# Cosine linear attention and a squared-ReLU MLP: batch 0's later queries behind w_in on GpSimd's queue, first products in halves of depth, casts on GpSimd, a new order

## The chip, the cores and the metric

The kernel runs on one core of a Trainium2 chip. The metric is the time in microseconds on the device; several runs give a median, and one further run is recorded by the profiler. Names of engines: PE is TensorE (PEld its weight loads), DVE is VectorE, ACT is ScalarE, POOL is GpSimd, SP is SyncE.

## The reference

```python
batch, n_heads, seq, head_dim = (8, 8, 576, 64)
pos = np.arange(S); theta = np.pi / 2.0 * pos / S
def phi(x, c, s):
    r = np.maximum(x, 0.0)
    return np.concatenate([r * c, r * s], axis=-1)
q_p, k_p = phi(q, cos, sin), phi(k, cos, sin)
kv = np.einsum('bhsf,bhsd->bhfd', k_p, v)
z = np.sum(k_p, axis=2)
num = np.einsum('bhsf,bhfd->bhsd', q_p, kv)
den = np.einsum('bhsf,bhf->bhs', q_p, z)[..., None] + 1e-06
x = (num / den).transpose(0, 2, 1, 3).reshape(B * S, H * D)      # 4608 x 512
h = np.maximum(x @ w_in, 0.0)                                    # w_in 512 x 2048
out = (h * h) @ w_out                                            # w_out 2048 x 512
```

Inputs and output are float32; the products run in bfloat16.

## The kernel before

The eight batches pass one after the other, each through an attention part and an MLP part, and the attention of later batches is interleaved with the MLP of earlier ones. A batch has 576 rows: four main tiles of 128 rows (j = 0 to 3; in the code J is 4) and a tail of 64 (j = 4). k, v and q of a batch are loaded in float32, one main transfer (1 MB, `load_main`, L355) and two tail transfers of 64 KB (`load_tail`, L363) each. There is one buffer for each of k, v and q.

*Attention.* `declare_feature` (L507) makes relu(x) times cos or sin in bfloat16 (tiles kp and qp), on ACT (L406) or DVE (L408). `declare_v` (L520) casts v to bfloat16 (vx), on ACT or DVE (L413); a column of ones beside it gives the sum z. `declare_kz` (L530) forms kv and z on PE, `declare_num` (L605) multiplies the transposed query features with them and divides (den and x, L637 to L639). Queries and x are transposed on PE for batches 0 and 1 (L591, L682) and by DMA on SP's queue later (L575, L667).

*MLP.* `declare_plain` (L712) is a group of the first product: 256 columns of the hidden layer (two blocks hb of 128) for half a batch's main rows (256 rows), eight matmuls of 256 columns, over the four blocks of depth. ACT takes the ReLU (rt, L416), DVE squares it into gT (L419). Batch 0 has 16 groups: hb = 0, 2, ... 14 for its first half of rows, then for its second. The first two groups are split by rows into matmuls of 128 columns, so that each 128 rows of x can start. From batch 3 on a form with seven products in place of eight takes over (`declare_seven1`, L810), with sums of blocks on DVE (w1s, xs; L427). `declare_rows` (L998) is batch 0's second product with w_out (w2sb), in steps of two hidden blocks for each of four row tiles, 64 matmuls of 512 columns; later batches use `declare_pair` (L922), seven products with sums gs and w2s.

*Loads of the start.* `prologue` (L1069) issues on SP: k, k's tail, q's first half (tiles 0 and 1), v's tail, v in two halves of heads, q's second half (tiles 2 and 3), q's tail. GpSimd's queue waits for v's tail by a one-element copy (L1090) and then issues w_in in quarters of 512 hidden columns (L373), which are cast to bfloat16 on the way. Then, on the same queue: batch 1's q and its tail, w_out's first quarter (L380), batch 1's k, w_out's second quarter, batch 1's v, the other quarters of w_out, batch 2's loads, and batch 0's two stores. Batches 3 to 7 load through SP. PE gets filler matmuls (`fill`, L1094) in the start, which write to a spare bank.

*What sets the order.* Operations are not issued as declared: a planner (`Planner`, L52 to L230) has a cost for each operation on each engine it may run on, due times (`pos`, `late`), buffers and a model of the loads, lays all on a time line, and the instructions are written out in that order (L1303 on), so every engine's stream is fixed when the program is built. `SHIFTS` (L21) moves single operations' due times or ties them to one engine. For the first loads the planner is given landing times by hand:

```python
for i in range(4):
    given([("w1", i)], 11.7 + 0.01 * i, size=2.6)
```

In `Planner.plan` a transfer's end follows from those planned before it:

```python
pipe = max(o.end + o.land, pipe) + o.size
o.done = pipe + (self.margin if e != "GIVEN" else 0.0)
```

An engine works through its stream in turn; what waits holds back what is behind it on that engine.

Of the kernel before, what the change touches and what calls it, by code (L numbers as in the profile page):

```python
# [21 lines left out]
23:9.5:ACT 37:-0.5 38:1.0 44:17.5:ACT 46:-1.0 53:-0.5 62:11.5 79:-2.0 85:-2.5 89:3.0 93:11.0  # L22
108:5.5 144:9.0 152:-2.0 157:9.5:ACT 191:-5.0 194:-1.0 202:-1.5 203:-3.5:ACT 204:2.0 210:3.0
238:2.5 241:2.5 243:5.0 249:-6.0 257:-4.0 260:-2.0 261:-6.0 270:2.5 271:3.5 287:-5.0 325:-2.0
335:-0.5 340:1.5 348:8.5 354:-7.0 364:-19.0 383:1.0 390:-3.5 392:1.0 417:-4.5 487:-5.0 492:1.5
516:-7.5 517:-5.5 530:39.0 533:25.5 546:9.0 563:5.5 565:12.5 573:-8.5 575:5.0 588:13.0 593:4.5
598:-2.0 611:-4.5 617:-5.5 636:-1.5 670:7.5 677:-2.0 690:1.0 698:0.0:DVE 702:22.5 703:-19.5
704:3.5:ACT 706:-4.0 715:2.0 731:-2.5 748:5.0 781:-4.5 783:-6.0 785:-7.0 787:-2.0 790:-1.0
794:-1.5 797:1.0 799:1.0 807:11.0 813:-5.5 817:-4.0 820:-7.0 822:-5.5 836:-3.5 850:-3.5
859:-34.0 860:-15.0 870:1.0 872:-4.0 884:12.0 890:49.0 893:17.0 906:5.5 907:23.5 911:3.0 917:3.0  # L30
936:-3.0 951:-12.5 957:-1.0 958:-1.5 963:-3.5 985:7.0 990:-4.0 998:3.5 1005:-4.5 1009:5.5
1023:-10.0 1024:-8.5 1030:-10.0 1041:-26.0:ACT 1042:-10.5 1133:-13.0 1143:1.5 1155:4.0 1157:3.0
1176:-4.5 1191:4.5 1209:5.5 1247:2.5 1306:-0.5
# [200 lines left out]
def kernel(  # L234
# [191 lines left out]
    def sub(out, in0, in1, op=ALU.subtract):  # L426
        nc.vector.tensor_tensor(out=out, in0=in0, in1=in1, op=op)  # L427
# [18 lines left out]
    T1, T2, t = {}, {}, 16.4  # L446
# [11 lines left out]
    def declare_load(b, nm, eng, pos=None, after=()):  # L458
        src = {"k": k, "v": v, "q": q}[nm]
        queue = nc.sync if eng == "SP" else nc.gpsimd  # L460
        for part, fn, cost, size, held in (
            (nm, load_main, 0.65 if eng == "SP" else 0.9, 3.1 if eng == "SP" else 2.7, 5.8),
            (nm + "t", load_tail, 1.3, 0.42, 6.8),
        ):
            buf = loaded[part, b] = plan.buf(part)

            def load(_, fn=fn, buf=buf):
                fn(src, nm, buf.i, b, queue)

            add((eng, cost), load, w=[buf], pos=pos, size=size, after=after, held=held if eng == "SP" else None)  # L470
# [49 lines left out]
    def declare_v(b, j, engs):  # L520
        buf = cached(vxb, (b, j), "vx" if j < J else "vxt")
        n = 1 if j < J else 0.65
        cost = {"ACT": 0.52 * n, "DVE": 0.34 * n}

        def cast(eng):
            copy(eng, at(buf)[:, :, 0:D], piece("v", b, j))
# [815 lines left out]
```

## Time and profile before

| what | value |
|---|---|
| runs | 277.44, 277.49 (median), 277.59 us |
| profiled execution | 276.82 us |
| its span | 274.8 us |
| granted TensorE clock | 1.0 throughout |
| first product with w_in on PE | 16.45 us from the span's start |
| first product with w_out on PE | 33.5 us |
| last product on PE | ends at 271.4 us |
| DMA: one quarter of w_in, issue to landing (median) | 10.5 us |
| DMA: one quarter of w_out, issue to landing (median) | 11.6 us |
| ACT cast of v, 128x512 | 26 at 636 ns |
| DVE cosine feature of q, 128x512 | 29 at 492 ns |
| DVE product of two bfloat16 tiles, 128x1024 | 686 ns |

All times inside the execution count from the span's start. "Busy" is the time in which an engine executes; waiting, and issuing DMAs, is not counted, except that GpSimd's DMA instructions stand among its busy time. In a timeline, a line has the start, the length, the engine, the kernel's line, the operation, what it writes and reads, its shape and how many are merged; in brackets is the idle time of the engine ahead of it, and what ended that. In a table of stretches the columns are: the stretch, its length, busy time of PE, PEld, DVE, ACT and POOL (with instruction counts), the granted clock, the mean share of the DMA engines, GB/s.

### The profile page before, as it was taken

The page shows a single profiled execution, that of the slowest core. Times are in us where ns is not written, and L with a number is a line of the kernel's source. Part 1 is how long each engine was busy: PE and PEld are TensorE (multiplying, and loading weights), DVE is VectorE, ACT ScalarE, POOL GpSimd, SP SyncE. Part 2 cuts the span into 40 slices and gives each one's busy share as a digit, 9 for nine tenths or more (in the row PEclk, how much of TensorE's full clock was granted, in tenths as well). Part 3 has the DMA queues.
Part 4 walks back from the last instruction along what each step waited for, and adds up shares of the span by engine and source line. Part 5 has one row for each costly group of instructions (what it writes and reads, how often), then busy time and mean ns, then how long its engine had stood idle before and what let it go on. Part 6 is the DMA issues. An engine that isn't in the chain of part 4 may idle for free.

```text
span 274.8 us, 7115 instructions
## 1 busy us (share of the span) xinstructions
PE 267.9 (98%) x2845; PEld 227.6 (83%) x2845; DVE 218.9 (80%) x515; ACT 194.9 (71%) x391; POOL 21.6 (8%) x38
## 2 busy tenths in 40 slices
PE   8979999999999999999999999999999999999994
PEld 3668856789988988888888898988988888888884
DVE  1789996997694989699968999799968798279652
ACT  3876982997895598589957994699735954684522
POOL 1453544010000000000000000000000000000000
PEclk9999999999999999999999999999999999999999
DMA  7999999969979998899299955996198301200025
GB/s 217 321 205 290 296 283 365 219 218 225 361 160 186 281 334 156 224 347 221 81 164 308 259 181 102 265 338 217 35 205 170 91 2 44 95 16 2 1 79 153
DMA packets 81840, 53.01 MB, mean 193 GB/s; under 512 B 53584, under 2 KB 77648, under 8 KB 81808
## 3 DMA queue, kind: packets, MB, share of 16 engines
q1 hardware_dynamic: 75136, 40.12, 58.4%
q0 software_dynamic: 6528, 12.32, 17.1%
q8 instruction: 22, 0.36, 0.5%
q10 hardware_dynamic: 144, 0.13, 0.1%
q14 instruction: 10, 0.08, 0.1%
HBM read 36.70 MB, written 9.44 MB: 168 GB/s over the span
## 4 chain that ended last, share of the span: by engine, by line
PE 80%; DMA 8%; DVE 7%; issue 1%; SPq 1%; POOL 1%; ACT 1%; DVEq 0%
PE banks L430 79%; DMA w1sb<-in_moe_w_in_dram 4%; DMA qpT<-qp 2%; DMA vt<-in_v_dram 2%; DVE rs L422 2%; DVE gT L419 2%; DVE gs L427 2%; PE banks L591 1%; DVE x L639 1%; POOL w1sb L373 1%; SPq L366 0%; PE banks L682 0%; DVE qp L408 0%; DVE kp L408 0%; SPq L358 0%
## 5 line engine op out<-in xcount | busy, mean ns | idle before, releaser
L430 PEld LDWEIGHTS <-w1sb 128*128 128x128 bf16 x784 | 73.0, 98 | 10.4 <-DMA w1sb<-in_moe_w_in_dram 1.4
L430 PE MATMUL banks<-xT,w1sb 128*128 128x256 bf16 (+1 forms) x576 | 68.4, 267 | 1.0 <-DMA w1sb<-in_moe_w_in_dram 1.0
L430 PEld LDWEIGHTS <-gs 128*128 128x128 bf16 x512 | 49.0, 98 | 5.9 <-DVE gs L427 0.2
L416 ACT ACTIVATE rt<-banks 128x512 bf16<-128x512 f32 x64 | 37.2, 600 | 14.9 <-PE banks L430 9.3
L430 PEld LDWEIGHTS <-gT 128*128 128x128 bf16 x400 | 38.0, 98 | 9.0
L430 PE MATMUL banks<-w2sb,gT 128*128 128x256 bf16 (+1 forms) x288 | 44.2, 296 | 0.0
L430 PEld LDWEIGHTS <-w1s 128*128 128x128 bf16 x320 | 30.7, 98 | 3.7
L430 PE MATMUL banks<-w2sb,gs 128*128 128x256 bf16 x256 | 33.0, 273 | 0.0
L430 PE MATMUL banks<-w2s,gs 128*128 128x256 bf16 x256 | 32.2, 273 | 0.0
L422 DVE CUSTOM_DVE_ANT_0 rs<-banks,sums 128x512 bf16<-128x512 f32 x40 | 27.0, 684 | 4.5 <-ACT sums L847 3.1
L419 DVE TENSOR_TENSOR gT<-rs 128x1024 bf16<-128x1024 bf16 (+1 forms) x50 | 27.7, 579 | 1.8 <-ACT rs L416 1.0
L416 ACT ACTIVATE rs<-banks 128x512 bf16<-128x512 f32 x40 | 23.6, 604 | 3.1 <-PE banks L430 2.9
L430 PE MATMUL banks<-xs,w1s 128*128 128x256 bf16 x160 | 23.0, 273 | 0.0
L430 PE MATMUL banks<-xT,w1s 128*128 128x256 bf16 x160 | 22.9, 273 | 0.0
L419 DVE TENSOR_TENSOR gT<-rt 128x512 bf16<-128x512 bf16 x48 | 19.2, 418 | 4.5 <-ACT rt L416 4.3
L427 DVE TENSOR_TENSOR ysb<-banks,sums 128x256 f32<-128x256 f32 x32 | 13.4, 418 | 11.2 <-PE banks L430 7.3
L406 ACT ACTIVATE qp<-q,sin_col 128x512 bf16<-128x512 f32 x31 | 22.1, 738 | 0.1
L639 DVE TENSOR_TENSOR x<-banks,den 128x512 bf16<-128x512 f32 x30 | 20.7, 691 | 1.0
L406 ACT ACTIVATE kp<-k,sin_col 128x512 bf16<-128x512 f32 x30 | 21.2, 734 | 0.0
L427 DVE TENSOR_TENSOR gs<-gT 128x1024 bf16<-128x1024 bf16 x28 | 19.2, 686 | 1.1 <-PE banks L430 0.7
L413 ACT CAST vx<-v 128x512 bf16<-128x512 f32 x26 | 16.2, 636 | 0.9 <-DMA v<-in_v_dram 0.9
L637 DVE TENSOR_SCALAR den<-banks 128x8 f32<-128x8 f32 (+1 forms) x38 | 6.0, 159 | 12.5 <-PE banks L430 12.3
(106 smaller groups left out, 364.0 us busy)
## 6 DMA issues: line engine op xcount, KB each, us to landing
out_dram<-ysb SPq DMA_DIRECT2D x13, 512.0 KB, 3.5
k<-in_k_dram SPq DMA_DIRECT2D x6, 1024.0 KB, 6.4
v<-in_v_dram SPq DMA_DIRECT2D x5, 1024.0 KB, 7.9
q<-in_q_dram SPq DMA_DIRECT2D x5, 1024.0 KB, 9.3
w1sb<-in_moe_w_in_dram POOLq DMA_DIRECT2D x4, 512.0 KB, 10.5
q<-in_q_dram POOLq DMA_DIRECT2D x2, 1024.0 KB, 11.2
w2sb<-in_moe_w_out_dram POOLq DMA_DIRECT2D x4, 512.0 KB, 11.6
k<-in_k_dram POOLq DMA_DIRECT2D x2, 1024.0 KB, 11.3
```

The costliest lines, as they stand in the source:

```text
L373: nc.gpsimd.dma_start(out=w1sb[:, :, f0:f1], in_=moe_w_in[:, f0:f1].rearrange("(kb p) f -> p kb f", p=P),)
L406: nc.scalar.activation(out=dst, in_=src, func=ACTF.Relu, scale=col)
L413: (nc.scalar.copy if eng == "ACT" else nc.vector.tensor_copy)(out=out, in_=in_)
L416: nc.scalar.activation(out=out, in_=in_, func=ACTF.Relu)
L419: nc.vector.tensor_tensor(out=out, in0=in_, in1=in_, op=ALU.mult)
L422: nc.vector._custom_dve(TENSOR_ADD_SAT, out=out, in0=in0, in1=in1, s0=float("inf"), s1=0.0)
L427: nc.vector.tensor_tensor(out=out, in0=in0, in1=in1, op=op)
L430: nc.tensor.matmul(out=out, lhsT=lhsT, rhs=rhs, start=start, stop=stop, skip_group_check=True)
L591: nc.tensor.transpose(t[:, h, :], qp_at(b, j)[:, h, :], ident[:, :])
L637: nc.vector.tensor_single_scalar(out=d, in_=n4[:, :, :, D], scalar=EPS, op=ALU.add)
L639: nc.vector.tensor_tensor(out=x_at(b, j).rearrange("p (b k) (l d) -> p b k l d", b=n, l=2), in0=n4[:, :, :, 0:D].rearrange("p b (k l) d -> ...
```

## The change

- *Loads.* SP no longer loads batch 0's q tiles 2 and 3 and the q tail. GpSimd's queue loads w_in in four eighths and two quarters, and q's second half and tail stand behind the first two eighths. The key of a w_in piece (`w1_key`) follows the new pieces.
- *First products.* Batch 0's first two groups are split into three parts each: the first half of depth for all 256 rows, then the second half of depth for each 128 rows.
- *Casts.* `declare_v` may cast on GpSimd (a multiplication by 1.0, twice), and from batch 2 on does nothing else; the cosine features of q may run on ACT as well as on DVE.
- *Stores.* Batch 0's two stores go through SP.
- *Planner.* The costs, sizes and given landing times are other numbers; a load of q on SP follows those of the k and v tails; batch 3's loads are declared k, v, q; `SHIFTS` is another list.

In the built program DVE has 500 instructions instead of 515, ACT 376 instead of 391, and PE 2836 matmuls instead of 2846 (two fillers and eight products fewer). 9 cosine features of k and 9 of q (128x512) move from DVE to ACT. GpSimd has 30 casts, 24 of 128x512 and six tails. On PE's stream the first two products with w_out now stand ahead of the last four groups with w_in; before, all 16 groups stood ahead of the first.

```diff
-    T1, T2, t = {}, {}, 16.4
+    T1, T2, t = {}, {}, 15.2
...
-        cost = {"ACT": 0.52 * n, "DVE": 0.34 * n}
+        cost = {"ACT": 0.52 * n, "DVE": 0.34 * n, "POOL": 0.75 * n}
 
         def cast(eng):
-            copy(eng, at(buf)[:, :, 0:D], piece("v", b, j))
+            if eng == "POOL":
+                nc.gpsimd.tensor_scalar(
+                    out=at(buf)[:, :, 0:D], in0=piece("v", b, j), scalar1=1.0, scalar2=1.0, op0=ALU.mult, op1=ALU.mult
+                )
+            else:
+                copy(eng, at(buf)[:, :, 0:D], piece("v", b, j))
...
+    def w1_key(hb):
+        return ("w1", hb // 2 if hb < 8 else 2 + hb // 4)
...
-        for c in range(2) if split else (None,):
+        whole = (0, KB, 0, TP, 0.0)
+        parts = [whole]
+        if split and b == 0:
+            parts = [(0, KB2, 0, TP, 0.0), (KB2, KB, 0, P, 4 * PROD1), (KB2, KB, P, TP, 4.5 * PROD1)]
+        elif split:
+            parts = [(0, KB, 0, P, 0.0), (0, KB, P, TP, PROD2)]
+        for k0, k1, c0, c1, later in parts:
...
     def st_name(b):
-        return "SP" if b >= 1 else "POOL"
+        return "SP" if b >= 0 else "POOL"
...
-    def declare_att(b, kpos, npos, cos_k=BOTH, cos_q=DVE1, cast=ACT1):
+    def declare_att(b, kpos, npos, cos_k=BOTH, cos_q=BOTH, cast=("POOL",)):
...
-    SPARE, SPARE_UNTIL = 5, 16.0
+    SPARE, SPARE_UNTIL = 5, 14.0
...
-            (k, "k", 0), (k, "kt", 0), (q, "q", 0), (v, "vt", 0), (v, "v", 0), (v, "v", 1), (q, "q", 1), (q, "qt", 0)
+            (k, "k", 0), (k, "kt", 0), (q, "q", 0), (v, "vt", 0), (v, "v", 0), (v, "v", 1)
...
         nc.gpsimd.tensor_copy(out=w1sb[0:1, 0, 0:1], in_=mem["vt"][0:1, 0, 0, 0:1])
-        for i in range(4):
+        for i in range(2):
+            load_w1(i, 8)
+        load_main(q, "q", 0, 0, nc.gpsimd, [slice(J // 2, J)])
+        load_tail(q, "q", 0, 0, nc.gpsimd)
+        for i in range(2, 4):
+            load_w1(i, 8)
+        for i in range(2, 4):
             load_w1(i, 4)
...
-        ([(L("v"), 1)], 12.15), ([(L("q"), 1)], 14.2), ([L("qt")], 14.6),
+        ([(L("v"), 1)], 12.3), ([(L("q"), 1)], 16.7), ([L("qt")], 17.1),
     ):
         given(keys, t, lat=0.0)
-    for i in range(4):
-        given([("w1", i)], 11.7 + 0.01 * i, size=2.6)
+    for i, t in enumerate((13.9, 15.2, 18.4, 19.7, 22.3)):
+        given([("w1", i)], t, lat=0.0)
+    given([("w1", 5)], 20.1, size=2.6)
...
-    declare_att(2, T2[1], [T2[1] + 1.7 + 1.75 * i for i in range(NS)], BOTH, BOTH, BOTH)
-    for nm in "qkv":
+    declare_att(2, T2[1], [T2[1] + 1.7 + 1.75 * i for i in range(NS)], BOTH, BOTH, ("POOL",))
+    for nm in "kvq":
         declare_load(3, nm, "SP", after=[turned["q", 2, J // 2]])
...
-    t0 = {"PE": 8.0, "ACT": 6.3, "DVE": 6.3, "SP": 10.0, "POOL": 12.9, "GIVEN": 0.0}
+    t0 = {"PE": 8.0, "ACT": 6.3, "DVE": 6.3, "SP": 10.0, "POOL": 16.0, "GIVEN": 0.0}
```

## The prediction

> **What bounds the kernel now.** I read the page's first part and a table of stretches first, to see whether TensorE (PE) ever waits; then its waits in order of time; then the DMAs that end them.
>
> ```profile
> PE 267.9 (98%) x2845; PEld 227.6 (83%) x2845; DVE 218.9 (80%) x515; ACT 194.9 (71%) x391; POOL 21.6 (8%) x38
> ```
>
> ```profile
> 16.45:33.50 17.05, 16.03 (x185) 14.19 (x184) 15.28 (x43) 12.45 (x23) 9.34 (x13) 1.00 1.16 272
> 33.50:100.00 66.50, 66.48 (x750) 53.85 (x748) 53.98 (x138) 51.84 (x101) 7.75 (x11) 1.00 0.99 262
> 100.00:200.00 100.00, 99.46 (x1114) 88.26 (x1112) 89.65 (x203) 81.45 (x170) 0.00 (x0) 1.00 0.85 209
> 200.00:271.40 71.40, 71.33 (x680) 63.46 (x679) 51.16 (x106) 37.85 (x80) 0.00 (x0) 1.00 0.29 75
> ```
>
> After the stretch and its length come the busy times of PE, PEld, DVE, ACT and POOL, the clock, the DMA share and GB/s. From the first product with w_in (16.45) to 33.5 PE idles 1.02 us; from there to the last product (271.4) 0.02 + 0.54 + 0.07 = 0.63 us in all. So the kernel is bound by PE: it can win little over 1.6 us and an earlier start, and it can lose whatever makes PE wait. DMA is full (share over 1) until 33.5. These are PE's lines around the change:
>
> ```profile
> 16.48 0.61 PE L430 MATMUL banks<-xT,w1sb 128*128 128x128 bf16 x8
> 19.64 1.05 PE L430 MATMUL banks<-xT,w1sb 128*128 128x256 bf16 x8 [0.86 <-DMA w1sb<-in_moe_w_in_dram]
> 22.19 1.05 PE L430 MATMUL banks<-xT,w1sb 128*128 128x256 bf16 x8 [0.16 <-DMA w1sb<-in_moe_w_in_dram]
> 23.52 8.90 PE L430 MATMUL banks<-xT,w1sb 128*128 128x256 bf16 x80
> 32.34 0.32 PE L430 MATMUL banks<-kvz,sums 128*64 128x65 bf16 x8
> 32.59 1.05 PE L430 MATMUL banks<-xT,w1sb 128*128 128x256 bf16 x8
> 33.48 2.75 PE L430 MATMUL banks<-w2sb,gT 128*128 128x512 bf16 x12
> ```
>
> The second and third quarters of w_in land at 19.6 and 22.1 and PE waits for both. Then it does all remaining first products before it touches w_out, at 33.48. GpSimd's queue shows when the later transfers land, since an issue on it waits for the transfer eight places before:
>
> ```profile
> 25.03 0.76 POOL L380 DMA_DIRECT2D w2sb<-in_moe_w_out_dram  x1 [1.70 <-DMA w1sb<-in_moe_w_in_dram]
> 28.45 0.89 POOL L358 DMA_DIRECT2D v<-in_v_dram  x1 [2.66 <-DMA q<-in_q_dram]
> 31.23 1.52 POOL L380 DMA_DIRECT2D w2sb<-in_moe_w_out_dram  x2 [0.64 <-DMA w2sb<-in_moe_w_out_dram]
> ```
>
> The last quarter of w_in lands at 25.0, batch 1's q at 28.4, the first quarter of w_out at 31.2: in order of issue, and 2.3 us before PE needs the last.
>
> [...]
>
> **The change part by part.** Profiled, before takes 276.82 us (span 274.8 and 2.0 around it); its runs' median, 277.49, is 0.67 higher. I add differences to both.
>
> *Loads.* Q rows 2, 3 and tail leave SP's queue (issues of 0.51 and 2.43 us, with nothing behind them until a transpose at 51) and go behind the first two eighths of w_in on GpSimd's. GpSimd then issues for about 6.9 us from 9.12 (two pieces at 0.8, q at 0.9, two tails at 0.62, four pieces at 0.8) instead of 3.2. That ends at 16, well before the data of the last quarter can move, so it is hidden. The bytes up to the end of w_in are the same and DMA is full, so the third quarter stays near 22.2 and the last near 25. Smaller runs may cost up to 0.6, a shorter mix may give 0.3: I take 25.1.
>
> *First products.* Halves of depth turn 32 products of 128 columns into 8 of 256 and 16 of 128: by 1.05 us for 8 wide and 1.06 for 16 narrow ones, 0.1 less. They start when half of x is there (its copies end at 15.4), about 1 us earlier. But PE then waits for the queries: q lands after 1 MB of w_in instead of beside it, near 16.7; features (0.48 to 0.73), transposes, copies of 1.0 and num follow, to about 19.6. So by 22.2 the same four groups (hb 0 to 6) are done; besides, the transposes of x and of the q tail, which before did at 23.07 and 23.29, come ahead. That gains about 0.4. By itself it would bring the end forward by this.
>
> *The order that goes with it.* In the changed program PE's instructions after this are: eight groups of w_in, 64 products; then two products with w_out, which wait for its first quarter; then the four groups with the last quarter of w_in, 32 products; then the q tail's num. Before had 15 of its 16 groups, and then the last, ahead of w_out. PE takes instructions in turn, so the two products hold back 3.5 us of work whose weights landed at 25. From 22.6 (third quarter, the copies of x ready) 64 products at 8.90/80 = 0.111 take 7.1 us: PE asks for w_out at 29.7. On GpSimd's queue, though, w_in's last quarter and batch 1's whole q are still ahead of it; only the q tail went behind it (128 KB, about 0.35 us at the rates shown). So it lands at 31.2 - 0.35 + 0.1, about 31.0; from 30.2 to 31.8 with the bounds above. PE idles about 1.3 us. Then two products (0.44), 32 (3.5) and num (0.25) end at 35.2. Before reaches the same state (62 w_out products left) at 33.48 + 0.44 = 33.9. **The start costs 1.3 us** (0.5 to 2.1), the gain of 0.4 already spent in it. The later quarters of w_out are asked for at 38 and after; before they landed by about 37, 42 and 45 (GpSimd's later waits and the landing times of 10.7 to 12.5), so they don't bind.
>
> *Casts.* 26 casts on ACT (16.2 us at 636 ns, and 2.1 for tails) and several on DVE become 30 on GpSimd, 24 of them full, from batch 2 on. ACT takes 18 cosine features (0.72 each, 13.0) that DVE loses (0.48 each, 8.6). ACT gets about 2 us lighter. [...] I take 0.2 us on PE (-0.6 to +3). The kz products wait for the casts; before, casts came up to 10 us ahead of them, and GpSimd has nothing else to do then.
>
> *Stores and the rest.* Batch 0's two stores go to SP, between transposes that went at 51.1 and 60.2; their rows are done by 55.5, so 4.6 us of slack hide them. New orders of loads on SP, k and v before q, have the same bytes; the chains to their features are several us long. At nothing, with the idle time above as the only gain. The end (3.4 us after the last product) stays.
>
> Sum: 1.3 + 0.2 = 1.5, so 278.3 for the profiled execution and **279.0** for a median like the one given.
>
> **Rivals.** *Waiting disappears* (not slower): w_out's first quarter lands before 29.7. That is the point from which it decides: then PE goes through at 29.7 + 4.2 = 33.9, level with before, and the freed ACT time removes up to 0.63 us later: 277.1, between 276.8 and 277.6. For it: earlier issues on GpSimd, and an order that places the two products there. Against: the bytes ahead are the same, DMA was full, and 6.2 us lay between the ends of the last quarter of w_in and this piece; the piece would have to gain 1.5 us. [...] between 150 and 165 DVE and ACT are already nearly always busy:
>
> ```profile
> 150.00:165.00 15.00, 15.00 (x161) 13.52 (x160) 14.76 (x30) 15.00 (x31) 0.00 (x0) 1.00 0.88 230
> 180.00:200.00 20.00, 20.00 (x218) 17.76 (x217) 19.47 (x41) 17.37 (x38) 0.00 (x0) 1.00 0.73 181
> ```
>
> [...] Against it: PE shows no idle time in these stretches even so, and ACT is relieved. [...]
>
> **How the numbers follow.** Forecast 55% (its own range 277.7 to 280.1), no waiting 25%, starved 20% (280.1 to 283). What a measurement can tell from no change is about 0.2%, 0.55 us: 276.9 to 278.0. Half of the second case is faster than that, half within it; of the forecast 6% lies within. So faster 0.13, same 0.19, slower 0.68. The range 276.9 to 281.0 leaves out about half of the starved case and the best of the second.
>
> **What would show it.** In the trace of the changed kernel: a wait of PE of 0.5 to 2 us at its first w_out product, named as a DMA of w2sb, ending at 30.2 to 31.8, with 64 products directly ahead of it; first w_in products near 15.5; third quarter at 22.2. PE's idle time from 36 to the end near 0.8. [...] I am wrong if PE passes that product without a wait, if w_out's first quarter lands elsewhere, or if PE idles over 1.5 us after 36.

## The result, and the profile after

| | kernel before | changed kernel |
|---|---|---|
| median, interleaved on one chip | 277.54 us (277.44 to 278.85) | 281.89 us (281.31 to 282.08) |
| profiled execution / its span | 276.82 / 274.8 us | 282.08 / 280.3 us |
| 62 products with w_out left on PE | 33.92 us | 37.47 us |
| from there to the start of PE's last product | 237.14 us | 238.52 us |
| from that to the end of the span | 3.7 us | 4.3 us |

The ratio is 1.0142 with an interval of 1.0108 to 1.0176: slower, above the range of 276.9 to 281.0. The direction was right, the size wrong by 2.9 us. Ratios leave out executions over 1.5% above the fastest of their kernel, which takes six of run 2's twenty below (282.55 to 284.52 us; with them its ratio is 1.012) and one of run 4's, while the medians given are of all. The span grew by 5.5 us: 3.55 in the start, 1.38 between the start and the last product, 0.57 after it. The 3.55 is at the upper end: in this execution and four others of kernels whose start is the same (runs 8, 9, 11 and 14 below) the state with 62 left comes at 36.3 to 37.5 us (middle 36.8), so that the start costs 2.4 to 3.55 (middle 2.9).

The page of the changed kernel, first line and busy times:

```profile
span 280.3 us, 7127 instructions
...
PE 269.1 (96%) x2829; PEld 226.7 (81%) x2835; DVE 216.3 (77%) x500; ACT 189.9 (68%) x376; POOL 45.1 (16%) x71
```

PE is hardly busier than before (267.9), but its share fell from 98% to 96%: the loss is waiting. The table of stretches says where (columns as before):

```profile
16.45:33.50 17.05, 14.09 (x153) 11.96 (x155) 12.20 (x37) 10.37 (x20) 8.11 (x12) 1.00 1.19 263
33.50:100.00 66.50, 66.12 (x734) 53.23 (x738) 54.36 (x137) 49.38 (x95) 15.26 (x24) 1.00 0.99 251
100.00:200.00 100.00, 99.04 (x1088) 86.80 (x1086) 87.64 (x194) 80.36 (x162) 13.43 (x19) 1.00 0.89 218
200.00:277.00 77.00, 76.27 (x754) 67.83 (x752) 54.18 (x111) 41.79 (x89) 0.00 (x0) 1.00 0.31 77
```

To 33.5 us PE idles 2.96 us instead of 1.02, and from 33.5 to 200 1.34 instead of 0.56, of which some 0.3 are matmuls that the trace lacks. (Of the last stretch, 0.7 us lie after the last product.) PE's timeline, the first product with w_in, and then from the third piece of w_in to the state that the table names:

```profile
16.91 1.03 PE L432 MATMUL banks<-xT,w1sb 128*128 128x256 bf16 x8
...
21.80 1.05 PE L432 MATMUL banks<-xT,w1sb 128*128 128x256 bf16 x8 [0.72 <-DMA w1sb<-in_moe_w_in_dram]
...
24.62 7.15 PE L432 MATMUL banks<-xT,w1sb 128*128 128x256 bf16 x64
33.19 0.39 PE L432 MATMUL banks<-w2sb,gT 128*128 128x512 bf16 x1 [1.43 <-DVE gT L421]
33.63 3.66 PE L432 MATMUL banks<-xT,w1sb 128*128 128x256 bf16 x32
37.22 0.32 PE L432 MATMUL banks<-kvz,sums 128*64 128x65 bf16 x8
37.47 1.47 PE L432 MATMUL banks<-w2sb,gT 128*128 128x512 bf16 x6
```

The order is as foretold: 64 products, the first with w_out, 32 products, num. The 64 start 2.0 us later than I had put them (22.6), and the wait of 1.43 us is put down to DVE's square gT, not to a DMA of w2sb. The first product with w_in, forecast near 15.5, comes at 16.91 (before: 16.48). x is late here: DVE's copy of kv and z (kvz) stands behind a cast of v that waits for the load of v's second half. DVE in the kernel before, then in the changed one:

```profile
11.84 0.43 DVE L413 CAST kvz<-banks 128x260 bf16<-128x260 f32 x1 [0.31 <-PE banks L430]
```

```profile
13.16 0.58 DVE L415 CAST vx<-v 128x512 bf16<-128x512 f32 x1 [1.22 <-DMA v<-in_v_dram]
13.66 0.41 DVE L415 CAST kvz<-banks 128x260 bf16<-128x260 f32 x1
```

In this execution that costs little, since PE waits for w_in at 21.8 all the same; what it would cost with w_in on time was not tried by itself. GpSimd's queue dates the later transfers, an issue that waits for a DMA about 0.3 us after its landing; in both traces that DMA is the one eight places earlier on this queue (the 17th here, at 27.17, waits for the 9th):

```profile
19.60 0.90 POOL L360 DMA_DIRECT2D q<-in_q_dram  x1 [3.12 <-DVE qpt L410]
...
27.17 0.64 POOL L368 DMA_DIRECT2D kt<-in_k_dram  x1 [1.69 <-DMA w1sb<-in_moe_w_in_dram]
29.71 0.77 POOL L368 DMA_DIRECT2D kt<-in_k_dram  x1 [1.90 <-DMA q<-in_q_dram]
32.31 0.76 POOL L382 DMA_DIRECT2D w2sb<-in_moe_w_out_dram  x1 [1.83 <-DMA w2sb<-in_moe_w_out_dram]
```

By the landings themselves, w_in's third quarter comes at 24.30 us (before: 22.14), its last at 26.89 (24.74), batch 1's q at 29.4 (28.2), w_out's first quarter at 32.0 (30.9). DVE's timeline shows what the square stood behind:

```profile
26.57 0.76 DVE L421 TENSOR_TENSOR gT<-rt 128x512 bf16<-128x512 bf16 x2
29.45 1.28 DVE L410 TENSOR_SCALAR qp<-q,cos_col 128x512 bf16<-128x512 f32 x3 [2.12 <-DMA q<-in_q_dram]
30.64 0.42 DVE L421 TENSOR_TENSOR gT<-rt 128x512 bf16<-128x512 bf16 x1
```

DVE stands 2.12 us on batch 1's q, with squares queued behind the features; ACT stands 1.77 us on the same transfer, with ReLUs behind. So at 31.8, when PE asks, the square is late, although w_out lands only 0.2 us after that.

What DMA does shows in the last two columns of two stretches, share and GB/s: the kernel before, the changed one, and run 14 below, which has the same loads at the start.

```profile
8.00:12.00 4.00, 4.00 (x50) 2.58 (x49) 3.15 (x9) 3.69 (x8) 3.06 (x5) 1.00 1.09 359
17.00:20.00 3.00, 2.14 (x40) 1.93 (x38) 2.39 (x7) 1.73 (x3) 2.36 (x5) 1.00 1.24 204
```

```profile
8.00:12.00 4.00, 3.78 (x32) 2.19 (x32) 3.33 (x8) 2.10 (x5) 2.85 (x4) 1.00 0.96 278
17.00:20.00 3.00, 2.76 (x41) 2.49 (x41) 1.82 (x6) 2.35 (x5) 0.40 (x1) 1.00 1.30 174
```

```profile
8.00:12.00 4.00, 3.78 (x47) 2.49 (x46) 2.91 (x9) 3.19 (x6) 3.36 (x5) 1.00 1.13 305
17.00:20.00 3.00, 1.82 (x30) 1.47 (x27) 1.62 (x5) 2.61 (x5) 0.98 (x2) 1.00 1.36 187
```

Two things differ. SP's last early load is now issued by 7.34 (before 9.93), and GpSimd, which waits for v's tail, issues its first at 9.44. Between them DMA runs short: from 8 to 12 us its share is 0.96 instead of 1.09, some 0.5 us of work. (GB/s can't be set against each other here: the trace counts 512 KB for a quarter of w_in, whose float32 values are 1 MB, so it counts the bytes after the cast.) And from 17 to 20 us, where most of what moves is w_in, DMA moves 174 GB/s with eighths at a share of 1.30, where it moved 204 at 1.24 with quarters. In the ten profiled executions whose loads are those of the changed kernel it is 174 to 199, in the seven with the loads as before 204 to 208. At 174 instead of 204 GB/s half of w_in, 1.05 MB as counted, would take 6.0 instead of 5.1 us: an estimate of 0.9 from these two figures. The rest of the 2.15 us is not accounted for. Run 14 is not short from 8 to 12, and its last quarter still comes at 25.7, 1.0 later than before.

### The profile page after: what moved, and what is told of

Read it like the earlier page. It is cut to its first block, busy times and chain, and to the rows that moved or that the text cites. A ratio compares the mean times of both kernels' runs of the same rounds, so it can differ in the third digit from the quotient of the medians.

```text
span 280.3 us, 7127 instructions
## 1 busy us (share of the span) xinstructions
PE 269.1 (96%) x2829; PEld 226.7 (81%) x2835; DVE 216.3 (77%) x500; ACT 189.9 (68%) x376; POOL 45.1 (16%) x71
## 3 DMA queue, kind: packets, MB, share of 16 engines
HBM read 36.70 MB, written 9.44 MB: 165 GB/s over the span
## 4 chain that ended last, share of the span: by engine, by line
PE 66%; DMA 14%; DVE 12%; SPq 3%; issue 2%; POOL 1%; ACT 1%; DVEq 0%; ACTq 0%
PE banks L432 66%; DMA q<-in_q_dram 8%; DVE gT L421 3%; DMA k<-in_k_dram 2%; DMA qt<-in_q_dram 2%; DMA vt<-in_v_dram 2%; SPq L368 1%; DVE rs L424 1%; DVE qp L410 1%; DVE gs L429 1%; DVE w2s L429 1%; DVE kp L410 1%; SPq L360 1%; DVE x L647 1%; POOL w1sb L375 1%
## 5 line engine op out<-in xcount | busy, mean ns | idle before, releaser
L432 PEld LDWEIGHTS <-gT 128*128 128x128 bf16 x400 | 37.7, 98 | 11.3 <-DVE gT L421 2.2
L421 DVE TENSOR_TENSOR gT<-rs 128x1024 bf16<-128x1024 bf16 (+1 forms) x50 | 29.2, 605 | 3.1 <-ACT rs L418 2.1
L424 DVE CUSTOM_DVE_ANT_0 rs<-banks,sums 128x512 bf16<-128x512 f32 x40 | 26.9, 684 | 5.4 <-ACT sums L864 4.7
L418 ACT ACTIVATE rs<-banks 128x512 bf16<-128x512 f32 x40 | 22.8, 605 | 3.8 <-PE banks L432 3.7
L421 DVE TENSOR_TENSOR gT<-rt 128x512 bf16<-128x512 bf16 x48 | 20.5, 445 | 5.6 <-ACT rt L418 5.4
L408 ACT ACTIVATE qp<-q,sin_col 128x512 bf16<-128x512 f32 x30 | 20.9, 724 | 3.5 <-DMA q<-in_q_dram 3.5
L530 POOL TENSOR_SCALAR vx<-v 128x512 bf16<-128x512 f32 x24 | 17.7, 766 | 25.9 <-DMA v<-in_v_dram 25.9
L429 DVE TENSOR_TENSOR gs<-gT 128x1024 bf16<-128x1024 bf16 x28 | 19.9, 712 | 2.0 <-PE banks L432 1.5
L530 POOL TENSOR_SCALAR vxt<-vt 128x256 bf16<-128x256 f32 x6 | 2.9, 482 | 92.4 <-DMA vt<-in_v_dram 63.5
```

What stands on the lines that cost most here:

```text
L408: nc.scalar.activation(out=dst, in_=src, func=ACTF.Relu, scale=col)
L418: nc.scalar.activation(out=out, in_=in_, func=ACTF.Relu)
L421: nc.vector.tensor_tensor(out=out, in0=in_, in1=in_, op=ALU.mult)
L424: nc.vector._custom_dve(TENSOR_ADD_SAT, out=out, in0=in0, in1=in1, s0=float("inf"), s1=0.0)
L429: (nc.gpsimd if eng == "POOL" else nc.vector).tensor_tensor(out=out, in0=in0, in1=in1, op=op)
L432: nc.tensor.matmul(out=out, lhsT=lhsT, rhs=rhs, start=start, stop=stop, skip_group_check=True)
```

## The experiments

Each is one edit of the changed kernel, unless it says otherwise. "Moved" means that operations, by their planner number, are taken out of the built order and written behind another: `move(ops, (moved,), behind)`. A ratio is to the kernel before, run beside it; the changed kernel's is 1.0142.

**1. Quarters instead of eighths.**

```diff
-        for i in range(2):
-            load_w1(i, 8)
+        load_w1(0, 4)
         load_main(q, "q", 0, 0, nc.gpsimd, [slice(J // 2, J)])
         load_tail(q, "q", 0, 0, nc.gpsimd)
-        (two eighths, two quarters)
+        (three quarters)
```

> The changed kernel with w_in in whole quarters again: first quarter, then q's second half and tail, then the other three, all on GpSimd's queue; order and all else as in the changed kernel. Theory short runs (eighths move slower, 3.45 us for the second pair against 2.55 for a quarter before): w_in's last quarter lands about 0.9 us earlier than in the changed kernel (26.0), and the time falls by 0.5 to 1, to about 281. Theory idle queue (w_in is late because q left SP's queue): no change beyond 0.3 us, the last quarter stays near 26.9.

282.01 us, 1.0124 (1.0069 to 1.0179). w_in's last quarter lands at 25.3, as the theory of short runs has it, and PE reaches the state with 62 products left at 35.97, 1.5 us before the changed kernel; yet the time is the same, since the rest took 240.5 us instead of 238.5. The first sign that a gain at the start is given back.

**2. The queries on SP, w_in in eighths.** `(q, "q", 1), (q, "qt", 0)` go back to the end of SP's list.

> The changed kernel with q's second half and tail loaded through SP again, w_in still in four eighths and two quarters. Theory idle queue (SP's queue runs dry from 8 to 12 us and GpSimd's issues start late): w_in's last quarter lands near 24.8 to 25.3 and the time falls by about 2 us, to 279.8. Theory short runs: the last quarter stays over 26 and the time falls by under 1 us.

281.15 us, 1.0092 (1.0064 to 1.0121). w_in's last quarter lands at 25.1, as the theory of the idle queue has it. Each of runs 1 and 2 alone brings it back into the range of the loads as before (24.65 to 25.8), each in one profiled execution, so they don't tell the two theories apart. In run 2 PE also idles for 1.38 us at 16, and its clock falls; run 3 shows the same more shortly.

**3. All the start's loads as before.**

```diff
+            ..., (v, "v", 1), (q, "q", 1), (q, "qt", 0)
...
-        (eighths, q, quarters)
+        for i in range(4):
+            load_w1(i, 4)
```

> The changed kernel with all loads of the start as before (q on SP, w_in in quarters); halves of depth, order and casts as in the changed kernel. Both theories of late w_in: last quarter at 24.7, the start's loss falls from 3.5 us to about 1.3 (the wait at the first w_out product, until 31 us), time 279.7. If the late w_in has another cause (the changed kernel's PE or VectorE order), it stays over 281.

280.89 us, 1.0104 (1.0028 to 1.0181). w_in lands as before (24.65), batch 1's q at 27.2, w_out at 29.7; no wait at the first w_out product is left. But the state with 62 left comes at 36.0 all the same, in part for a reason that I had not looked for. In this kernel's stretches, the column before the last two is the granted clock:

```profile
16.00:17.00 1.00, 0.03 (x1) 0.00 (x1) 0.97 (x4) 0.93 (x3) 0.00 (x0) 0.90 1.22 204
17.00:18.00 1.00, 1.00 (x5) 0.72 (x6) 0.42 (x2) 1.00 (x3) 0.03 (x1) 0.50 1.26 215
18.00:19.00 1.00, 1.00 (x8) 0.75 (x6) 0.00 (x0) 0.07 (x1) 1.00 (x2) 0.50 1.24 202
19.00:20.00 1.00, 1.00 (x12) 1.00 (x11) 0.55 (x2) 0.00 (x0) 0.64 (x1) 0.50 1.25 208
```

PE is busy for 0.65 us of the microsecond before these and 0.03 of the first, and its clock falls to half, by the means of these slices and the next (0.89) from 16.8 to 20.2; in run 2 from 16.2 to 23.0.

**4. The kernel before, with casts on GpSimd** from batch 2 on, at the places where they stood.

```diff
+            if b >= 2:
+                nc.gpsimd.tensor_scalar(...)
+            else:
+                copy(eng, at(buf)[:, :, 0:D], piece("v", b, j))
```

> The kernel before with one part alone: its casts of v of batches 2 to 7 run on GpSimd, at the same places of the order; nothing else is moved. Theory [...]: slower by 1 to 3 us, with the products of two bfloat16 tiles longer by 25 ns or more in the mean. Rival (the loss after 37 us comes from the new order, not the casts): within 0.5 us of before, or faster by up to 0.6 as ScalarE has 26 casts less.

279.41 us, 1.0043 (1.0011 to 1.0074). So the casts alone cost some 1.2 us (0.3 to 2.1 by the interval) where nothing else had been arranged for them. Where the time goes is not known.

**5 and 6. The two causes of the wait at w_out, one by one.** 5: `move(ops, (224,), 142)`, the two w_out products behind the last four groups of w_in. 6: `move(ops, (176, 180, 184, 188, 177, 181), 123)`, six q features of batch 1 behind the square that the product reads.

> The changed kernel, with its first two products with w_out put behind the four groups with the last quarter of w_in; nothing else moves. In the changed kernel TensorE waits 1.43 us at these products while the four groups' weights have been there for 6 us. Theory (the place of the two products holds back 3.5 us of ready work): the wait goes, the state with 62 w_out products left comes at 36.1 instead of 37.5, the time falls by 1.2 to 1.5 us to about 280.5. Rival (what holds the start back is the stream of DVE and ACT, so that the squares for the last four groups come late too): the wait moves behind the groups and less than 0.5 us is won.

> The changed kernel, with the six q features of batch 1 on DVE and ACT put behind the square that the first w_out product reads; nothing else moves. Theory (the wait of 1.43 us at that product is a queue on DVE: the square stands behind features that wait for batch 1's q, landed at 29.4): the wait falls to what w_out's first quarter itself costs, 0.3 us (it lands at 32.0, TensorE asks at 31.8), and the time falls by about 1.1 us to 280.8. Rival (the reason on record, that TensorE waits for w_out's landing itself): no more than 0.3 us won, and the wait is then named as a DMA. Against both: batch 1's transposes at 38.8 come late, and what is won is lost there.

Run 5: 283.06 us, 1.0166 (1.0113 to 1.0218). The rival holds: the wait has moved on to the w_in groups, which need PSUM banks that ACT's ReLUs free, and those stand behind batch 1's q as well. PE of run 5:

```profile
24.44 7.15 PE L432 MATMUL banks<-xT,w1sb 128*128 128x256 bf16 x64
33.39 3.65 PE L432 MATMUL banks<-xT,w1sb 128*128 128x256 bf16 x32 [1.80 <-ACT rt L418]
```

Run 6: 281.08 us, 1.0104 (1.006 to 1.0147). The wait falls from 1.43 to 0.56 us and now ends as w_out lands (31.17, PE starts at 31.21), so the reason on record, w_out's landing, is worth that much once DVE's queue is out of its way. 0.92 us come back at 38, where the division of batch 0's q tail is late, and 0.87 at 83.

**7. Run 3 with filling products.**

```diff
+            if op.n == 98:
+                bk = next(b for b in op.bufs if b.pool == "F")
+                for _ in range(4):
+                    nc.tensor.matmul(out=bank(bk), lhsT=zeros[:, 0:P], rhs=zeros, start=True, stop=True)
```

> The variant with the start's loads as before (280.9 us), with four products of zeros of 512 columns, 0.22 us each, ahead of the first w_in product; their bank is written over by that product. In that variant TensorE idles 1 us at 16 to 17 and its granted clock then falls to 0.5 for some 3.4 us. Theory (the idle time drops the clock, the slow products cost 1.5 us, and the changed kernel has no filling products after 14 us, before had them to 16): the clock stays at 1.0, the state with 62 w_out products left comes at 34.5 instead of 36.0, the time falls by 1.5 to about 279.4. Rival (the clock falls whatever TensorE does, or its loss is hidden by the landing of w_in): the same 280.9.

280.91 us, 1.013 (1.0093 to 1.0167). The clock stays at 1.0, as expected; the time does not follow. In the profiled execution w_in landed 1 us later than in run 3 (25.6), and PE waited 0.77 us at w_out again.

**8. Casts that I took for others.** `move(ops, (534, 537), 548)` with these casts on ACT.

> The changed kernel, with two of batch 4's four casts moved from GpSimd to ACT, at a place where ACT is idle 1.0 us. In the changed kernel three DVE operations beside the four casts take 1.08, 1.09 and 0.82 us instead of 0.69, 0.69 and 0.42, and TensorE waits 0.22 and 0.33 us behind them, at 135 us. Theory [...]: two of the three take their usual 0.69 and 0.42 us, and TensorE's two waits at 135 fall from 0.55 to under 0.25 in sum, start to start from 0.88 to under 0.5. Rival (the new order of DVE's work makes these waits): both stay as they are. In the whole time the 0.4 us is at the edge of what can be told.

283.17 us. A miss: these are batch 4's casts, which run at 100 us; the ones at 131 are batch 5's. They came late on ACT and cost a wait of 1.55 us at 109. Run 11 below is the one that was meant.

**9. ACT's features behind the copies.** `move` (478) behind 402, (550) behind 585, (702) behind 639, (553, 555) behind 597.

> The changed kernel; on ACT five features of q and k of batches 3 to 5 are put behind the PSUM copies that followed them; nothing else moves. Theory for the rest of the kernel (ACT's new features wait in turn for transfers, 0.8 us for batch 3's q, which lands at 83.1 and before landed at 76.8, and copies that TensorE waits for stand behind them): TensorE's waits for ACT at 83 to 84, 112 and 124 (0.26 to 1.03 us in the runs so far, the first) vanish, the time from the state with 62 w_out products left to the last product falls by 0.7 to 1.2 us, the whole to 280.7 to 281.2. Rival (the rest loses its 1.4 us to the casts alone, or to many small shifts): no change beyond 0.3 us, new waits of the same size nearby.

283.03 us, 1.0163 (1.0118 to 1.0208). The wait at 82 to 85 is still there, 0.77 us, now named as DVE's: DVE's features of the same q stand ahead of DVE's copies. So it isn't ACT's order alone.

**10. Both moves of 5 and 6, and six w_in sums on DVE** `(506, 511, 512, 513, 510, 515)` behind 179.

> The changed kernel with three moves in the order: the two w_out products behind the last four groups of w_in, batch 1's six q features behind the square for w_out, and six w_in sums on DVE, which batch 3 is the first to need, behind batch 1's first copies. Theory (the start waits because features that wait for batch 1's q stand on DVE and ACT ahead of squares and ReLUs that free TensorE's banks; each of the two moves alone met the other's wait, or DVE's lateness at 38): TensorE goes without a wait from the 64 products on, 11.3 us from their start to the state with 62 products left instead of 12.9, and no wait over 0.3 us at 38; the time falls by about 1.5 us less what is given back at 83, to 280.5 to 281.0. Rival (the wait only wanders on, as in the two runs before it): under 0.5 us won.

282.12 us, 1.0151 (1.0115 to 1.0186). 12.3 us from the 64 products to the state with 62 left, not 11.3: 0.87 us of waiting for ACT's ReLUs remain. The sums that I had put off then held up a cast of v, and PE waited 1.76 us at 45.

**11. Batch 5's casts**, two of the four: `move(ops, (704, 707), 720)`, on ACT. The changed kernel's DVE beside all four casts, GpSimd's casts, and what PE waits for:

```profile
132.22 1.08 DVE L421 TENSOR_TENSOR gT<-rs 128x1024 bf16<-128x1024 bf16 x1
133.22 1.09 DVE L429 TENSOR_TENSOR gs<-gT 128x1024 bf16<-128x1024 bf16 x1
134.24 0.82 DVE L421 TENSOR_TENSOR gT<-rs 128x512 bf16<-128x512 bf16 x1
```

```profile
131.08 3.71 POOL L530 TENSOR_SCALAR vx<-v 128x512 bf16<-128x512 f32 x4 [5.07 <-DMA v<-in_v_dram]
```

```profile
135.12 0.39 PE L432 MATMUL banks<-w2sb,gT 128*128 128x256 bf16 x2 [0.22 <-DVE gT L421]
135.84 1.92 PE L432 MATMUL banks<-w2s,gs 128*128 128x256 bf16 x16 [0.33 <-DVE gs L429]
```

> The changed kernel, with two of batch 5's four casts moved from GpSimd to ACT, at a place where ACT is idle 1.0 us (an earlier run meant these and moved batch 4's). Theory [...]: of the three DVE operations at 132 to 135 that take 1.08, 1.09 and 0.82 us beside the four casts, the latter two take 0.69 and 0.42, and TensorE's starts at 134 to 136 lose under 0.4 us instead of 0.88. Rival (the order of DVE's work makes these waits): all as they are.

DVE of run 11; its two casts on GpSimd end at 133.7:

```profile
133.21 1.08 DVE L421 TENSOR_TENSOR gT<-rs 128x1024 bf16<-128x1024 bf16 x1
134.21 0.68 DVE L429 TENSOR_TENSOR gs<-gT 128x1024 bf16<-128x1024 bf16 x1
134.81 0.41 DVE L421 TENSOR_TENSOR gT<-rs 128x512 bf16<-128x512 bf16 x1
```

The operation that still has a cast beside it takes 1.08 us, the other two their 0.68 and 0.41, and PE's two waits at 135 are gone. The theory holds: these DVE operations last longer where a cast runs beside them, by 0.40 us here (1.08 against 0.68) and by 0.41 (0.82 against 0.41) in the changed kernel. (283.10 us in one run; the two casts made a copy on ACT late, 0.48 us at 139.)

**12. All at once:** run 7 with the moves of 9, 10 and 11.

> All at once: the start's loads as before, four filling products ahead of the first w_in product, and the moves of the runs on ACT's copies, on the freed start and on batch 5's casts. Theory (late w_in, the queue on batch 1's q, ACT's features ahead of copies and the casts beside DVE's sums are the whole loss): what is left is TensorE's eight products that before had done earlier, so that the time is within 0.7 us of before's, 277.4 to 278.1. Rival (a further loss that these do not touch): 279 or more. It would beat the kernel before only if the casts and ACT's load had been worth something in themselves.

282.47 us, 1.0165 (1.012 to 1.0209). The rival holds: PE starts the rest at 35.75 instead of 37.47 and takes 240.3 us for it instead of 238.5, with waits of 1.08 (at 43), 0.96 (84) and 0.59 us (138).

**13 to 15. A common root?** 13: the moves of 5 and 6, and thirteen w_in sums put where DVE had idle time. 14: `move` (358, 360) behind 361 on SP, the tails of batch 3's k and v behind its q, with their features (469, 470) and cast (471) behind q's features. 15: both, on run 7.

> The changed kernel with w_out's first products behind the last four groups, batch 1's q features behind the square for w_out, and thirteen w_in sums (0.33 us each on DVE, first needed at 116 us) put into stretches at 47, 73 and 87 us in which DVE has idle time. Theory (the start is bound by DVE's stream: it stands on batch 1's q and then works off a backlog, so that a wait taken away comes back where DVE is late next): with 4.3 us taken out of the stretch from 24 to 46 no wait over 0.5 us is left at 31 to 46, and the state at batch 1's first kz products (43.3 to 45.4 in the runs so far) comes by 1.3 us or more earlier than in the changed kernel; the time falls by 0.5 to 1.3 us, the rest given back at 83. Rival (many small causes): a new wait of 1 us or more before 46.

> The changed kernel; batch 3's tails of k and v are loaded behind its q instead of ahead of k, as before loaded them, and the features and the cast of these tails go behind q's features; nothing else moves. Theory (batch 3's q lands late because four tail issues stand ahead of it on SP's queue, and features waiting for it hold up ACT's and DVE's copies): q lands at about 80.3 instead of 83.1, and TensorE's wait at 82 to 85 (0.3 to 1.1 us in every run so far) is gone without a new one before 100; the time falls by 0.3 to 0.9 us. Rival (this stretch is bound by ACT's load, whatever lands when): the wait stays at 0.3 or more.

> Both runs above in one, with the start's loads as before and four filling products. Theory (transfers that come late to engines that work in turn are the common root): what is left of the loss are the casts beside DVE's sums at 134 (0.9 us start to start) and the later start of some w_in products (0.8), so 1.0 to 1.7 us over before, about 279. Rival (many small causes): 281 or more, as all runs so far.

Runs 13 and 15: 282.86 us, 1.016 (1.012 to 1.0201), and 282.35, 1.0153 (1.0115 to 1.0192). From 31 to 46 only 0.87 us of waiting is left, but the sums that I had put at 47 made a division late: 1.76 and 3.19 us at 57 and 58. My placement, so that they decide nothing about the start.

Run 14: 280.51 us, 1.0093 (1.0062 to 1.0123), the lowest of all edits that keep the changed loads. SP's timeline of the changed kernel, and then of run 14:

```profile
67.73 1.32 SPq L368 DMA_DIRECT2D kt<-in_k_dram  x2
69.15 1.28 SPq L368 DMA_DIRECT2D vt<-in_v_dram  x2
70.52 0.56 SPq L360 DMA_DIRECT2D k<-in_k_dram  x1
71.17 0.53 SPq L360 DMA_DIRECT2D v<-in_v_dram  x1
71.75 1.50 SPq L360 DMA_DIRECT2D q<-in_q_dram  x1
```

```profile
67.41 0.53 SPq L360 DMA_DIRECT2D k<-in_k_dram  x1
68.12 0.45 SPq L360 DMA_DIRECT2D v<-in_v_dram  x1
68.62 1.52 SPq L360 DMA_DIRECT2D q<-in_q_dram  x1
```

Two pairs of tail issues ahead of k take 2.8 us. q is issued 3.1 us earlier and lands at 79.7 instead of 83.1 (before: 76.8). The stretch from 82 to 100, in run 14:

```profile
82.00:100.00 18.00, 18.00 (x200) 16.17 (x201) 12.99 (x31) 14.76 (x27) 2.29 (x4) 1.00 1.06 236
```

PE is busy for all of it (changed kernel: 17.91, so only 0.09 us is won here), and a wait of 0.28 us at 124 is gone as well. From the state with 62 left to the last product it takes 237.83 us instead of 238.52, 0.69 less, in one profiled execution of each.

**16 to 18. The start again, with batch 3's q forward.** 16: run 7 with 14. 17: run 14 with the move of 6 and (90), the q tail's division, behind 120. 18: both. In 17 and 18 the division stands ahead of the product whose result it should read, so that these rows are divided from what the bank held before; all instructions are there.

> The run that put batch 3's tails behind its q (280.5 us), and the start's loads as before with four filling products. Theory (late w_in is a loss of its own, and its gain was given back at 83): the state with 62 w_out products left at 34.7 to 36.2 instead of 36.3 to 37.5, no wait at 82 to 85, so 279.0 to 280.0. Rival (the start's loads are worth nothing, since DVE or w_out sets the end of the start): 280.5 again.

> The run that put batch 3's tails behind its q, with batch 1's six q features on DVE and ACT behind the square that the first w_out product reads, and the division of batch 0's q tail three operations earlier on DVE. Theory (DVE stands 2.1 us on batch 1's q, and the division was late only by its place): the wait at the first w_out product falls from 1.4 to about 0.5, none over 0.3 at 38, so 279.3 to 279.9. Rival (DVE's backlog comes out elsewhere): a new wait of 0.9 us or more before 60 and 280.5 again.

> Both: the start's loads as before with four filling products, batch 1's q features and the q tail's division moved, batch 3's tails behind its q. Theory: the waits that remain are the casts beside DVE's sums at 134 and what w_out's first quarter costs, 278.6 to 279.4, and not below the kernel before, since TensorE has eight w_in products more to do from 23.5 us on. Rival (the start is bound by what none of these touches): 280.5.

Run 16: 281.29 us, 1.0127 (1.0083 to 1.0171). State with 62 left at 36.09; no wait from 82 to 100; but after that PE waits for ACT at 111 (1.05 us), 125 (1.20) and 139 (0.74). ACT of run 16 shows on what:

```profile
106.22 0.72 ACT L408 ACTIVATE qp<-q,sin_col 128x512 bf16<-128x512 f32 x1 [2.13 <-DMA q<-in_q_dram]
...
123.74 0.72 ACT L408 ACTIVATE kp<-k,cos_col 128x512 bf16<-128x512 f32 x1 [1.48 <-DMA k<-in_k_dram]
```

It is the same picture, one batch and two batches later: features that wait for batch 4's q and batch 5's k, with PE's copies behind them. SP had batch 4's q behind a transpose that holds the queue for over 6 us:

```profile
92.80 6.62 SPq L583 DMA_TRANSPOSE qpT<-qp  x1
99.47 0.58 SPq L360 DMA_DIRECT2D q<-in_q_dram  x1
```

In the kernel before this q was issued at 91.4, with no transpose between it and k, and landed at 101.8; here at 106.1, in the changed kernel at 107.0. Runs 17 and 18: 281.43 us, 1.0146 (1.0098 to 1.0194), and 281.34, 1.0141 (1.0097 to 1.0184); PE waited 1.94 us for the misplaced division, so they say nothing about the start. In 17 the rest, once begun, took 237.17 us, as in the kernel before.

## Why the prediction was wrong, step by step

**Loads: the step that failed first.** "The bytes up to the end of w_in are the same and DMA is full, so the third quarter stays near 22.2 and the last near 25." The third came at 24.30 and the last at 26.89 in this execution; in the ten with the changed loads the last came at 25.7 to 27.2 (middle 26.2), in the seven with the loads as before at 24.65 to 25.8 (middle 25.4). So it is 0.8 us late as a rule and 2.15 in this one, where I had bounded the cost by 0.6. The traces show two causes. From 8 to 12 us DMA isn't full in this execution, as the queries had covered the time until GpSimd could issue: I had worked out when its issues end, and not whether something is under way when they begin. And w_in moves more slowly in eighths (174 against 204 GB/s from 17 to 20 us), for which alone I had allowed the 0.6, an estimate that no trace of before showed. Which has what share stays open: over the ten executions the share of DMA from 8 to 12 is 0.96 to 1.13, and runs 1 and 2, each of which changes one of the two, both land at 25.1 to 25.3. (I also took GpSimd's issues for the landings, so that my 25.0, 28.4 and 31.2 stand some 0.3 us late.)

**First products: failed with it.** The first product with w_in starts at 16.91 instead of 15.5, since x is late, for which the new order of DVE's instructions is to blame and not a load of w_in. Batch 0's queries land at 17.95 instead of 16.7, the first num of these rows begins at 20.66 where I had it done by 19.6, the third quarter comes 2.1 us late, and the 64 products start at 24.62 instead of 22.6. The gain of 0.4 never came. (Halves of depth themselves save 2.12 less 2.11 us by my figures, that is nothing, and not 0.1.)

**Order at w_out: right place, size near, cause wrong.** I had PE ask at 29.7 and w_out land at 31.0, a wait of 1.3; it asked at 31.8, w_out landed at 32.0, and it waited 1.43 us for DVE. DVE and ACT have batch 1's features ahead of the squares and ReLUs, and that q (29.4 instead of 28.2) stands behind the late w_in. I had looked at what is queued behind the waiting product on PE, and not at what stands on DVE and ACT ahead of its inputs. Run 5 shows that the product's place, which I had blamed, is no cause by itself; run 6 that the landing is worth about 0.5 us.

**The start's sum** was 1.3 (0.5 to 2.1) and measured 3.55: 2.0 by the late start of the 64 products, 1.43 by the wait, where I had 1.3 for it and 0.4 against it. In the four other executions with this start it measured 2.4 to 3.15, with waits of 1.42 to 1.63 us at w_out, so part of the 3.55 is this execution's.

**Casts: the effect was an estimate.** For all casts together I had allowed 0.2 us of PE (-0.6 to +3); before's trace has no cast of more than one element on GpSimd, so that this was my estimate, and not shown. A full cast takes 766 ns in the mean (0.75 us in the planner): 621 in the median, up to 1104 beside DVE. Of DVE's forms only some stretch beside a cast: squares and sums with two bfloat16 operands, 128x512 from 420 to 740 ns in the mean of five and 128x1024 from 690 to 871 in the mean of nine, and two of five features of k, which take 511 and 835 instead of 480. Operations that read PSUM do not: 685 and 683 ns for the two-input form with ReLU (L424), 692 and 691 for the division. Over the kernel that comes to some 3.6 us of DVE, so DVE got lighter all the same (218.9 to 216.3). ACT got lighter by 5.0 us, not by the 2 that I wrote (16.2 + 2.1 - 13.0 is 5.3). That the time came out among those of the rival "starved" (280.1 to 283), in which the casts make PE wait, is chance: in the changed kernel they cost PE under 1 us. What reaches PE in the changed kernel is one place, at 134 to 136: 0.55 us of waits, 0.88 by the starts of PE's products on both sides. Run 11 shows that the casts make it, though it lost 0.48 us elsewhere. In the kernel before, casts on GpSimd alone cost some 1.2 us (run 4).

**New orders of loads: "at nothing" failed.** Batch 3's q lands 6.3 us later than before, batch 4's q 5.2, batch 5's k 4.9, where the later start explains 3.55. ACT got features that wait for these transfers, ahead of copies that free PE's banks. Run 14 brings batch 3's q forward and needs 0.69 us less for the rest in its profiled execution, half of the 1.38 for which I had taken 0.2. PE's waits account for less of it: in the changed kernel it idles 0.09 us from 82 to 100 and 0.28 at 124, and in run 14 at neither. Most of what is left stands at 134 to 136, beside the casts. It was not taken apart further.

**What I said would prove me wrong:** w_out landing elsewhere (32.0, outside 30.2 to 31.8) and over 1.5 us of PE idle after 36 (by the stretches it is under 1.3 from there to 200, so that this sign alone would have missed the loss). Of what I said would show the forecast, the 64 products ahead of w_out came and the size of the wait (0.5 to 2 us); the first product at 15.5, the third quarter at 22.2 and the wait's name did not. (If the 6% is a part of the forecast's 55, my chances come to 0.125, 0.16 and 0.72, and not 0.13, 0.19 and 0.68.)

**What is shown and what is not.** Shown in traces: late w_in, though its two causes are not told apart; DVE's and ACT's queues behind batch 1's q; DVE's operations longer beside casts; late q of batch 3. In times, run 14 is 0.5% nearer to before than the changed kernel, runs 2 and 3 about 0.4 to 0.5%; these intervals overlap the changed kernel's, and runs 7 and 16, which join such edits, are no better. PE reached 62 left at 35.5 to 36.6 in runs 1, 3, 6, 7, 10, 12 and 16, up to 1.3 us ahead of the middle of the five executions with the changed start (36.8), and then needed 238.4 to 240.6 us, where before needed 237.14. My reading is that a gain at the start doesn't bring batches 3 to 5 forward as much as PE, so that PE meets their transfers earlier and waits; of the places where it would, only batch 3's was tried by itself (run 14). No version beat the kernel before. Open: what the new order at the start costs with w_in on time, how much the order of SP's transposes and loads of batches 4 and 5 costs (not tried by itself), what a start without misplaced work would give, and the 0.57 us after the last product: that stretch took 4.3 us in runs 1 and 6 too, and 3.6 in runs 2, 3 and 7.

## What to carry to other kernels

When a load is moved to another queue, see not only whether the new queue can issue in time, but what keeps the DMA engines busy in the gap that it leaves, and at what rate pieces of the new size move (here 174 GB/s where it was 204). For each wait that a late transfer causes, list what stands behind the waiting instruction on every engine that reads the transfer, DVE and ACT too: copies and ReLUs that free banks are PE's work at one remove (1.80 us of waiting in run 5). And when waits wander from run to run, suspect a pace set further up, here a queue on which loads stand behind transposes (one of 6.62 us in run 16).

## What the runs showed of the hardware that was not expected

TensorE's clock fell to half after less than 1 us of full idleness. In run 3 PE was busy for 0.65 us from 15 to 16 and for 0.03 from 16 to 17; then the clock was 0.50 for 3.4 us, and 8 products of 256 columns took 1.89 instead of 1.03 us. In run 2 it was 0.50 for 6.8 us, from 16.2 on, in an idle time of 1.38 us that began at 15.96. Four filling products in such a wait kept it at 1.0 in run 7, though run 7 won no time. And in the changed kernel it stayed at 1.0 through PE's wait of 1.43 us at 31.8, so what share of which stretch PE has to idle before the clock falls is not shown here.

A second observation: a DVE operation with two bfloat16 inputs and a GpSimd cast are longer beside each other, in the changed kernel by up to 0.40 us (128x1024: 0.69 to 1.09) and 0.48 us (128x512: 0.62 to 1.10), while a DVE operation of the same size that reads PSUM stays within 2 ns in the mean (683 beside a cast and 685 elsewhere, 691 and 692). A third: w_in in eighths (256 hidden columns) moved at 174 to 199 GB/s from 17 to 20 us, in quarters at 201 to 208; batch 0's last queries, which move among the eighths until 17.4 to 18.0, are not the reason, since run 2 has them on SP and shows 199 as well.
